# Weight preparation for the second layer in four smaller pieces, one block later, and small constants at other addresses

## The chip, the cores and the metric

The kernel runs on one core of a Trainium2 chip. The metric is the device time of one execution in microseconds (us); lower is better. The engines are named as in the profile: PE multiplies matrices (PEld loads its weights), DVE is the vector engine, ACT the scalar engine, POOL is GpSimd, SP issues the DMA transfers from one queue.

## The reference

Attention with pooled keys and values, and then two feed-forward layers with different gates. All arrays are float32.

```python
def _attn_ref(q, k, v):                      # (8, 8, 576, 64) each
    k_p = k.reshape(B, H, Sp, 8, D).mean(axis=3)
    v_p = v.reshape(B, H, Sp, 8, D).mean(axis=3)
    scores = scale * np.matmul(q, k_p.transpose(0, 1, 3, 2))
    attn = softmax(scores)                   # written out in the reference
    return np.matmul(attn, v_p)

def _moe_ref(x, w_in, w_out):                # x (4608, 512), w_in (512, 2048)
    h = x @ w_in
    g = np.where(h >= 1, h, np.where(h <= -1, 0.0, (h + 1) ** 2 / 4))
    return g @ w_out

def _moe2_ref(x, w_in, w_out):
    h = x @ w_in
    g = h - np.tanh(h)
    return g @ w_out

# out = _moe2_ref(_moe_ref(attention, w1_in, w1_out), w2_in, w2_out)
```

## The kernel before

**Tiling.** The first layer works through 12 blocks of 384 tokens (`TB`), each in 16 steps, one for each 128 of the 2048 hidden columns. Step t = 16 j + f is written "block j, step f" below. Each float32 operand is split into a high and a low half (`xh`/`xl`, `wh`/`wl`, `gh`/`gl`), so a product takes three matmuls: 12 of 384 columns for the hidden values `ph` (`h_mm`, L578) and, two steps later, 12 for the output `po` (`out_mm`, L623). Between them stands a chain over DVE and ACT: `g` is clipped (DVE L585, which is used below to mark the start of a step), squared (ACT L589), combined (DVE L593), and split into `gh` (ACT L601) and `gl` (DVE L602).

**Attention beside it.** While block j runs, the attention of block j + 1 is done, four pairs of heads at steps that a plan fixes. PE makes the scores `psc`, ACT the exponentials `ex` (L452), POOL divides them (L466) and splits a remainder `rr` (L474, L475), PE turns them (`pam`, `par`), ACT and DVE take them out of PSUM (`ah` L511, `al` L517, `ar` L509 and L510), PE multiplies with the values (`ppv`). For a new pair of batch and heads POOL pools the keys and values (`kvraw`, L315, then `bd`, L324 to L326) and PE turns them (`pkt`, L356), into a PSUM buffer that comes free with `al`. Per block this falls to four pairs in blocks 2, 5 and 8, to three in blocks 3, 6 and 9, and to one in blocks 4 and 7.

**Weight preparation for the second layer.** Sixteen units u. Unit u is loaded into `wraw` (`w_load`, L149 or L151, a buffer of which there is one), turned from a scaled bit layout into plain float32 in the staging tile `wf` (`conv`: ACT L159 and L160, DVE L164 to L166, once for each half i), and split into high and low (ACT L249, DVE L250). Even units also get four sums on POOL (L239 to L242, written back into `wraw`) and a second split, of these sums. The results go back to DRAM as `w2c` and `w2o`. The staging tile is the same buffer as `ost`, in which each block's output leaves for DRAM.

**What sets the order.** In the first layer's main loop the program only gives a priority: each step calls its functions in a fixed order, and the plan (`add(t, slot, ...)`) hangs the other work on steps. A scheduler then orders each engine's queue by its own reckoning, and a unit's work may stand steps before or behind the t of its plan. Engines run their queues in order. The second layer (from L875 on) has its order written out by hand, behind the first.

**Addresses.** The pool `const` holds the constants in the order in which they are asked for. When the first layer is over, its pools are given up and the second layer's tiles are laid over the same addresses from the start, in the order of the string `LAYOUT`: first `w0` (14336 bytes per partition), then `s0` (1024), a gap of 640, and so on. With `reuse_waits="tile"` a tile waits for the last users of the tiles that it covers, and of no others. `w0` takes the first weights `wc` of the second layer; `half`, the bias of ACT L589, is read in every step of the first.

Of the kernel before, what the change touches and what calls it, by code (L numbers as in the profile page):

```python
# [10 lines left out]
F32 = mybir.dt.float32  # L11
# [4 lines left out]
ALU = mybir.AluOpType  # L16
# [35 lines left out]
def attention_two_moe_kernel(  # L52
# [50 lines left out]


    kvraw = const.tile([P, 3, POOL * D], F32, tag="kvraw", name="kvraw")
    ident = const.tile([P, P], F32, tag="ident", name="ident")
    half = const.tile([P, 1], F32, tag="half", name="half")
    mask = const.tile([P, 2], F32, tag="mask", name="mask")

    third = const.tile([P, 16], F32, tag="third", name="third")[:, 0:1]  # L110

    vlrs = [const.tile([P, 2, P], F32R, tag=f"vlr{i}", name=f"vlr{i}") for i in range(6)]
    ars = [const.tile([P, TB], F32R, tag=f"ar{i}", name=f"ar{i}") for i in range(2)]
    n_vr = itertools.count()

    def constants(sel):
# [60 lines left out]
    def staging():  # L179
        t = sb.tile([P, KC * TB], I32, tag="ost", name="wf", bufs=1)  # L180
        return t[:, 0 : 2 * 512].rearrange("p (c m) -> p c m", m=512)

    def conv(r, a, s):
        conv_a(r, a, s)
        conv_v(r, a, s)
# [39 lines left out]
            w1_split_a(f)  # L225
            w1_split_v(f)

    def w2_prep(u):
        r, a = raws.pop((1, u)), staging()
        for i in (0, 1):  # L230
            conv(r[:, i], a[:, i], r[:, i, :, 0])
        af = a.bitcast(F32)
        r0, r1 = (r[:, i].rearrange("p m t -> p (m t)") for i in (0, 1))
        U[("w2", u)] = (r, af, r0, r1)
        if u % 2:
            return
        a11, a12, a21, a22 = (af[:, i, 256 * c : 256 * c + 256] for i in (0, 1) for c in (0, 1))
        c1, c2, c3, c4 = (r0[:, 256 * i : 256 * i + 256].bitcast(F32) for i in range(4))
        nc.gpsimd.tensor_tensor(c1, a21, a22, ALU.add)  # L239
        nc.gpsimd.tensor_tensor(c3, a11, a21, ALU.subtract)  # L240
        nc.gpsimd.tensor_tensor(c2, c1, a11, ALU.subtract)
        nc.gpsimd.tensor_tensor(c4, a12, c2, ALU.subtract)  # L242

    def w2_split(u):
        r, af, r0, r1 = U.pop(("w2", u))
        p = u // 2

        def split(x, hi):
            nc.scalar.activation(hi.bitcast(F32R), x, AF.Copy)  # L249
            nc.vector.tensor_tensor(x.bitcast(F32R), x, hi.bitcast(F32), ALU.subtract)  # L250

        if u % 2:
            split(af.rearrange("p i m -> p (i m)"), r0)
            for i in (0, 1):
                hi, lo = r0[:, 512 * i : 512 * i + 512].bitcast(F32), af[:, i]
                nc.sync.dma_start(out=w2o[2 * p + i][:, 0], in_=hi)
                nc.sync.dma_start(out=w2o[2 * p + i][:, 1], in_=lo)
            return
        split(af.rearrange("p i m -> p (i m)"), r1)
        for x, h in ((af.rearrange("p i m -> p (i m)"), 1), (r1.bitcast(F32), 0)):  # L260
            nc.sync.dma_start(out=w2c[p][:, h, 4:6], in_=x[:, 0:512].rearrange("p (m n) -> p m n", n=256))
            nc.sync.dma_start(out=w2c[p][:, h, 6], in_=x[:, 768:1024])
        split(r0.bitcast(F32), r1)
        for x, h in ((r0.bitcast(F32), 1), (r1.bitcast(F32), 0)):
            nc.sync.dma_start(out=w2c[p][:, h, 0:4], in_=x.rearrange("p (m n) -> p m n", n=256))


    xt = {}
# [538 lines left out]
    for f in range(FC):  # L807
        if f >= 2:
            add(FC + f - 2, "w", w1_split, f)
        if f:  # L810
            ahead("w", w_load, (1, f))
        t = FC + 8 * f + 5
        add(t, "w", w2_prep, f)
        add(t + 2, "w", w2_split, f)
        add(t + 3, "load2", used, "w")

    def go(t, *slots):
        for s in slots:
# [278 lines left out]
```

## Time and profile before

| | us |
|---|---|
| median of 3 runs (lowest, highest) | 1779.36 (1778.71, 1782.97) |
| time of the profiled execution | 1774.08 |
| its span from first to last instruction | 1772.3 |
| busy in the span: PE, DVE, ACT, POOL | 1726.8, 1075.9, 820.1, 335.3 |

The profile is one execution. Its span is cut into windows below at the starts of DVE L585, so that a window is a block of 16 steps. The ends of matmuls are modelled, and each overlaps the next, so an idle time of PE is read a little too short.

### The profile page before, as it was taken

The numbers are of one execution on the slowest core, as the hardware profiler recorded it, in microseconds if no ns is written. First come the engines' busy times: TensorE is split into PE (matmuls) and PEld (weight loads), VectorE is DVE, ScalarE is ACT, GpSimd is POOL, SyncE is SP. The second block draws the span as 40 slices with busy tenths as digits, with TensorE's granted clock in tenths as the row PEclk, the third lists the DMA queues.
The fourth block names the chain that finished last, engine by engine and source line by source line (L and its number), as shares of the span: only waits on it lengthen the run. The fifth ranks groups of instructions, "written<-read, shape, count | busy, mean of one in ns | idle before, by whom it ended". The sixth has DMA issues, their size and how long they took to land.

```text
span 1772.3 us, 27599 instructions
## 1 busy us (share of the span) xinstructions
PE 1726.8 (97%) x10224; PEld 1591.2 (90%) x10224; DVE 1075.9 (61%) x1993; ACT 820.1 (46%) x2014; POOL 335.3 (19%) x433
## 2 busy tenths in 40 slices
PE   8999989999999999999999899999999999999999
PEld 6569989899999999899999788998888988889887
DVE  7878876767676676755544445454545455555544
ACT  6656655555555455544432334343434344343433
POOL 5442243321433312431010010110101010101000
PEclk8999999999999999999999899999999999999999
DMA  8643242413343232420100664342434342424232
GB/s 248 212 131 96 88 143 82 151 47 122 101 123 124 75 122 75 131 59 10 28 25 19 254 262 147 105 153 96 143 107 144 107 143 96 154 97 154 95 119 95
DMA packets 162422, 207.59 MB, mean 117 GB/s; under 512 B 77808, under 2 KB 115696, under 8 KB 161264
## 3 DMA queue, kind: packets, MB, share of 16 engines
q1 hardware_dynamic: 162288, 205.84, 35.5%
q8 instruction: 80, 1.31, 0.3%
q14 instruction: 54, 0.44, 0.1%
HBM read 163.32 MB, written 41.94 MB: 116 GB/s over the span
## 4 chain that ended last, share of the span: by engine, by line
PE 76%; DVE 10%; DMA 5%; ACT 4%; POOL 3%; issue 2%; SPq 1%; ACTq 0%; DVEq 0%; POOLq 0%
PE y L993 23%; PE po L623 14%; PE ph L578 14%; PE bkX L928 9%; PE bkA L928 6%; PE bkZ L928 6%; DMA wraw<-in_moe_w_out_dram 2%; DVE gl L602 1%; PE psc L437 1%; DVE wf L166 1%; DVE g L585 1%; DVE wf L250 1%; DVE wraw L164 1%; POOL kvraw L315 1%; PE ph L571 1%
## 5 line engine op out<-in xcount | busy, mean ns | idle before, releaser
L993 PE MATMUL y<-wr,gh 128*128 128x512 f32 x1152 | 362.1, 395 | 0.0
L993 PEld LDWEIGHTS y<-wr,gh 128*128 128x128 f32 x1152 | 206.9, 188 | 39.6
L993 PE MATMUL y<-wr,gl 128*128 128x512 f32 x576 | 227.2, 394 | 0.0
L589 ACT ACTIVATE g<-g,half 128x384 f32<-128x384 f32 x192 | 118.8, 619 | 215.0 <-DVE g L585 214.7
L578 PE MATMUL ph<-xh,whl 128*128 128x384 f32 x704 | 197.7, 341 | 0.0
L623 PE MATMUL po<-gh,whl 128*128 128x384 f32 x704 | 195.7, 339 | 0.0
L928 PE MATMUL bkX<-xc,wc 128*128 128x256 f32 x1296 | 189.8, 282 | 0.0
L968 ACT ACTIVATE th<-c 128x512 f32<-128x512 f32 x144 | 91.1, 632 | 208.5 <-DVE c L961 116.1
L928 PEld LDWEIGHTS bkX<-xc,wc 128*128 128x128 f32 x1296 | 175.0, 190 | 6.0
L981 DVE TENSOR_TENSOR gl<-c,gh 128x512 fp32r<-128x512 f32 x144 | 104.7, 727 | 104.3 <-ACT gh L977 104.3
L971 DVE TENSOR_TENSOR c<-c,th 128x512 f32<-128x512 f32 x144 | 100.9, 701 | 95.6 <-ACT th L968 94.8
L602 DVE TENSOR_TENSOR gl<-g,gh 128x384 fp32r<-128x384 f32 x176 | 110.6, 629 | 74.9 <-ACT gh L601 73.7
L585 DVE TENSOR_SCALAR g<-ph 128x384 f32<-128x384 f32 x192 | 106.1, 553 | 77.2 <-PE ph L578 71.0
L593 DVE TENSOR_TENSOR g<-ph,g 128x384 f32<-128x384 f32 x192 | 106.4, 554 | 74.5 <-ACT g L589 73.0
L977 ACT ACTIVATE gh<-c 128x512 fp32r<-128x512 f32 x144 | 91.0, 632 | 114.2 <-DVE c L971 114.2
L895 POOL TENSOR_TENSOR xr<-xr 128x512 f32<-128x512 f32 x9 | 12.7, 1409 | 661.2 <-DMA xr<-x2d 593.2
L928 PE MATMUL bkA<-xc,wc 128*128 128x256 f32 x864 | 127.7, 284 | 8.1 <-DMA wc<-w2c 4.8
L928 PEld LDWEIGHTS bkA<-xc,wc 128*128 128x128 f32 x864 | 119.0, 192 | 15.0 <-DMA wc<-w2c 5.2
L993 PEld LDWEIGHTS y<-wr,gl 128*128 128x128 f32 x576 | 108.3, 188 | 26.0
L578 PEld LDWEIGHTS ph<-xh,whl 128*128 128x128 f32 x704 | 128.6, 188 | 0.3
L623 PEld LDWEIGHTS po<-gh,whl 128*128 128x128 f32 x704 | 128.8, 188 | 0.0
L601 ACT ACTIVATE gh<-g 128x384 fp32r<-128x384 f32 x176 | 91.9, 522 | 78.0 <-PE po L623 55.3
(156 smaller groups left out, 3672.6 us busy)
## 6 DMA issues: line engine op xcount, KB each, us to landing
wr<-w2o SPq DMA_DIRECT2D x144, 512.0 KB, 3.3
wraw<-in_moe_w_in_dram SPq DMA_DIRECT2D x32, 512.0 KB, 4.7
wraw<-in_moe_w_out_dram SPq DMA_DIRECT2D x32, 512.0 KB, 5.1
wc<-w2c SPq DMA_DIRECT2D x8, 1792.0 KB, 14.2
x2d<-ost SPq DMA_DIRECT2D x48, 192.0 KB, 1.9
out_dram<-yo SPq DMA_DIRECT2D x36, 256.0 KB, 4.5
w2c<-wraw SPq DMA_DIRECT2D x16, 512.0 KB, 2.6
kvraw<-in_k_dram SPq DMA_DIRECT2D x28, 256.0 KB, 2.9
```

The source lines that it names most:

```text
L578: nc.tensor.matmul(ps, a[:, cs], x[:, c, :], start=(i == 0), stop=(i == 3 * KC - 1))
L585: nc.vector.tensor_scalar(a, hp[t], -1.0, 1.0, ALU.max, ALU.min)
L589: nc.scalar.activation(a, a, AF.Square, bias=half, scale=0.5)
L593: nc.vector.tensor_tensor(a, hp.pop(t), a, ALU.max)
L601: nc.scalar.activation(gh, a, AF.Copy)
L602: nc.vector.tensor_tensor(gl, a, gh.bitcast(F32), ALU.subtract)
L623: nc.tensor.matmul(o, a, m, start=(f == 0 and i == 0), stop=(f == FC - 1 and i == len(ops) - 1))
L928: nc.tensor.matmul(o, w[:, wi, c], x[:, xi, c], start=new and i == 0, stop=i == 5, skip_group_check=not new)
L968: nc.scalar.activation(th, H[(n, i)], AF.Tanh)
L971: nc.vector.tensor_tensor(H[(n, i)], H[(n, i)], GG.pop((n, i, "t")), ALU.subtract)
L981: nc.vector.tensor_tensor(gl, H.pop((n, i)), gh.bitcast(F32), ALU.subtract)
L993: nc.tensor.matmul(Y[c], a[:, cs], b, start=first and i == 0, stop=last and i == 2)
```

## The change

The work on a unit is cut into smaller functions: `w2_conv` for each half, `w2_sums`, `w2_own` (the split of the unit itself), `w2_mixed` (the split of the sums) and `w2_rows` (the split of an odd unit). Its plan starts 13 steps later and runs over steps t, t + 2, t + 4 and, for even units, t + 6; the next load is planned for the last of them. No instruction on the engines is added or taken out, and no DMA. The tiles `vlrs` and `ars`, which the attention uses last in block 10, are asked for ahead of `ident`, `half`, `mask` and `third`, so that `w0` and `s0` lie over `kvraw`, `vlrs` and `ars`, and the gap of 640 bytes over the small constants.

```diff
     kvraw = const.tile([P, 3, POOL * D], F32, tag="kvraw", name="kvraw")
+    vlrs = [const.tile([P, 2, P], F32R, tag=f"vlr{i}", name=f"vlr{i}") for i in range(6)]
+    ars = [const.tile([P, TB], F32R, tag=f"ar{i}", name=f"ar{i}") for i in range(2)]
     ident = const.tile([P, P], F32, tag="ident", name="ident")
     half = const.tile([P, 1], F32, tag="half", name="half")
...
-    vlrs = [const.tile([P, 2, P], F32R, tag=f"vlr{i}", name=f"vlr{i}") for i in range(6)]
-    ars = [const.tile([P, TB], F32R, tag=f"ar{i}", name=f"ar{i}") for i in range(2)]
...
+    def w2_conv(u, i):
+        if i == 0:
+            U[("w2", u)] = staging()
+        r, a = w2_parts(u)[:2]
+        conv(r[:, i], a[:, i], r[:, i, :, 0])
...
+    def w2_halves(x, hi):
+        nc.scalar.activation(hi.bitcast(F32R), x, AF.Copy)
+        nc.vector.tensor_tensor(x.bitcast(F32R), x, hi.bitcast(F32), ALU.subtract)
...
+    def w2_own(u):
+        af, r0, r1 = w2_parts(u)[2:]
+        w2_halves(af, r1)
+        for x, h in ((af, 1), (r1.bitcast(F32), 0)):
+            nc.sync.dma_start(out=w2c[u // 2][:, h, 4:6], in_=x[:, 0:512].rearrange("p (m n) -> p m n", n=256))
+            nc.sync.dma_start(out=w2c[u // 2][:, h, 6], in_=x[:, 768:1024])
+
+    def w2_mixed(u):
+        r0, r1 = w2_parts(u)[3:]
+        w2_halves(r0.bitcast(F32), r1)
         for x, h in ((r0.bitcast(F32), 1), (r1.bitcast(F32), 0)):
-            nc.sync.dma_start(out=w2c[p][:, h, 0:4], in_=x.rearrange("p (m n) -> p m n", n=256))
+            nc.sync.dma_start(out=w2c[u // 2][:, h, 0:4], in_=x.rearrange("p (m n) -> p m n", n=256))
+        raws.pop((1, u))
...
-        t = FC + 8 * f + 5
-        add(t, "w", w2_prep, f)
-        add(t + 2, "w", w2_split, f)
-        add(t + 3, "load2", used, "w")
+        t = 2 * FC + 8 * f + 2
+        add(t, "w", w2_conv, f, 0)
+        add(t + 2, "w", w2_conv, f, 1)
+        if f % 2:
+            add(t + 4, "w", w2_rows, f)
+            add(t + 4, "load2", used, "w")
+        else:
+            add(t + 2, "w", w2_sums, f)
+            add(t + 4, "w", w2_own, f)
+            add(t + 6, "w", w2_mixed, f)
+            add(t + 6, "load2", used, "w")
```

How the queues change is shown at three places. In the changed kernel's rows the line numbers differ: L585, L593, L602 and L517 become L590, L598, L607 and L522; the conversions L159, L160 and L164 to L166 become L157, L158 and L162 to L164; the splits L249 and L250 become L247 and L248; POOL's L315, L466 and L242 become L320, L471 and L244.

**First place** (blocks 2, 5 and 8, steps 3 to 5). POOL's queue holds the sums of an even unit (`wraw`), the division of the exponentials (`ex`) and the pooling of keys and values (`kvraw`). Before:

```order
L240 TENSOR_TENSOR wraw<-wf 128x256
L241 TENSOR_TENSOR wraw<-wraw,wf 128x256
L315 TENSOR_TENSOR kvraw<-kvraw 128x3x256
L466 TENSOR_TENSOR ex<-ex,rc 128x432
L242 TENSOR_TENSOR wraw<-wf,wraw 128x256
L474 CAST rr<-ex 128x3x16
L315 TENSOR_TENSOR kvraw<-kvraw 128x3x128
```

After:

```order
L242 TENSOR_TENSOR wraw<-wf 128x256
L243 TENSOR_TENSOR wraw<-wraw,wf 128x256
L320 TENSOR_TENSOR kvraw<-kvraw 128x3x256
L244 TENSOR_TENSOR wraw<-wf,wraw 128x256
L320 TENSOR_TENSOR kvraw<-kvraw 128x3x128
L471 TENSOR_TENSOR ex<-ex,rc 128x432
L320 TENSOR_TENSOR kvraw<-kvraw 128x3x64
```

The fourth sum, which reads `wf` last, stood behind the division and now stands ahead of it, and the second pooling step goes ahead of the division too. DVE's queue at the same place, from step 3's `gl` to step 5's `ar`; before:

```order
L602 TENSOR_TENSOR gl<-g,gh 128x384
L585 TENSOR_SCALAR g<-ph 128x384
L593 TENSOR_TENSOR g<-ph,g 128x384
L602 TENSOR_TENSOR gl<-g,gh 128x384
L585 TENSOR_SCALAR g<-ph 128x384
L517 TENSOR_TENSOR al<-pam,ah 128x384
L593 TENSOR_TENSOR g<-ph,g 128x384
L510 CAST ar_132<-par 16x128
L250 TENSOR_TENSOR wraw<-wraw 128x1024
L510 CAST ar_132<-par 16x128
```

After:

```order
L607 TENSOR_TENSOR gl<-g,gh 128x384
L590 TENSOR_SCALAR g<-ph 128x384
L598 TENSOR_TENSOR g<-ph,g 128x384
L248 TENSOR_TENSOR wraw<-wraw 128x1024
L607 TENSOR_TENSOR gl<-g,gh 128x384
L590 TENSOR_SCALAR g<-ph 128x384
L522 TENSOR_TENSOR al<-pam,ah 128x384
L598 TENSOR_TENSOR g<-ph,g 128x384
L515 CAST ar_128<-par 16x128 x2
L607 TENSOR_TENSOR gl<-g,gh 128x384
```

The split of the sums (`wraw<-wraw`) stood in step 5, between two `ar`, and now stands in step 4, ahead of that step's `gl` and of the next `al`.

**Second place** (the same blocks, steps 7 to 9): the conversions of the next, odd unit and its split, DVE. Before:

```order
L164 SCALAR_TENSOR_TENSOR wraw<-wraw 128x512
L165 TENSOR_SCALAR wf<-wf 128x512
L602 TENSOR_TENSOR gl<-g,gh 128x384
L166 ISA wf<-wraw,wf 128x1024
L164 SCALAR_TENSOR_TENSOR wraw<-wraw 128x512
L585 TENSOR_SCALAR g<-ph 128x384
L165 TENSOR_SCALAR wf<-wf 128x512
L166 ISA wf<-wraw,wf 128x1024
L593 TENSOR_TENSOR g<-ph,g 128x384
L250 TENSOR_TENSOR wf<-wf,wraw 128x1024
L602 TENSOR_TENSOR gl<-g,gh 128x384
L585 TENSOR_SCALAR g<-ph 128x384
```

After:

```order
L162 SCALAR_TENSOR_TENSOR wraw<-wraw 128x512
L163 TENSOR_SCALAR wf<-wf 128x512
L590 TENSOR_SCALAR g<-ph 128x384
L164 ISA wf<-wraw,wf 128x1024
L464 TENSOR_SCALAR sm<-sm 128x6
L162 SCALAR_TENSOR_TENSOR wraw<-wraw 128x512
L598 TENSOR_TENSOR g<-ph,g 128x384
L466 RECIPROCAL rc<-sm 128x6
L163 TENSOR_SCALAR wf<-wf 128x512
L164 ISA wf<-wraw,wf 128x1024
L607 TENSOR_TENSOR gl<-g,gh 128x384
L590 TENSOR_SCALAR g<-ph 128x384
```

Each half of a unit has three conversion instructions (L164, L165, L166; L162 to L164 after). They stood in steps 7 and 8; now the first two stand at the end of step 6, the other four in step 7, and step 8, which begins with the last row shown of the change, holds only the split (`wf<-wf,wraw`). ACT's queue at that place, before:

```order
L601 ACTIVATE gh<-g 128x384
L452 ACTIVATE ex,sm<-psc,mx 128x72 x6
L589 ACTIVATE g<-g,half 128x384
L159 ACTIVATE wraw<-wraw 128x512
L160 ACTIVATE wf<-wraw 128x512
L601 ACTIVATE gh<-g 128x384
L159 ACTIVATE wraw<-wraw 128x512
L160 ACTIVATE wf<-wraw 128x512
```

After:

```order
L606 ACTIVATE gh<-g 128x384
L157 ACTIVATE wraw<-wraw 128x512
L158 ACTIVATE wf<-wraw 128x512
L457 ACTIVATE ex,sm<-psc,mx 128x72 x6
L157 ACTIVATE wraw<-wraw 128x512
L594 ACTIVATE g<-g,half 128x384
L158 ACTIVATE wf<-wraw 128x512
L606 ACTIVATE gh<-g 128x384
L247 ACTIVATE wraw<-wf 128x1024
```

The first conversions stood behind the six exponentials and now stand ahead of them.

**Third place** (SP, from the second to last block's output `x2d` to the first weights of the second layer, with what each waits for). Before:

```order
L633 DMA x2d_118<-ost 128x384 [waits DMAHW6_49,DVE_49]
L875 DMA wc_10510<-w2c_84 128x3584 [waits DMAHW7_49,Activation_49]
L633 DMA x2d_119<-ost 128x384 [waits DMAHW0_49,Activation_49]
L633 DMA x2d_119<-ost 128x384 [waits DMAHW1_49,DVE_49]
L633 DMA x2d_119<-ost 128x384 [waits DMAHW2_49,Activation_49]
L633 DMA x2d_119<-ost 128x384 [waits DMAHW3_49,DVE_49]
L875 DMA wc_10516<-w2c_85 128x3584 [waits DMAHW4_49,PE_49]
```

After:

```order
L638 DMA x2d_118<-ost 128x384 [waits DMAHW6_49,DVE_49]
L887 DMA wc_10510<-w2c_84 128x3584 [waits DMAHW7_49]
L638 DMA x2d_119<-ost 128x384 [waits DMAHW0_49,Activation_49]
L638 DMA x2d_119<-ost 128x384 [waits DMAHW1_49,DVE_49]
L638 DMA x2d_119<-ost 128x384 [waits DMAHW2_49,Activation_49]
L638 DMA x2d_119<-ost 128x384 [waits DMAHW3_49,DVE_49]
L887 DMA wc_10516<-w2c_85 128x3584 [waits DMAHW4_49,PE_49]
```

The order is the same; the load of `wc` into `w0` no longer waits for ACT.

## Rows read from the trace of the kernel before

**Rows 1.** The page's first line.
```profile
span 1772.3 us, 27599 instructions
```

**Rows 2.** Windows: five blocks; us, then busy us (instructions) of each engine.
```profile
135.18:214.29 79.11, 77.45 (x443) 73.87 (x442) 68.28 (x121) 54.98 (x142) 20.76 (x24) 1.00 0.33 101
454.43:535.95 81.52, 76.95 (x456) 75.15 (x455) 56.95 (x108) 42.71 (x124) 31.49 (x44) 1.00 0.38 114
535.95:617.87 81.92, 78.28 (x473) 75.85 (x472) 56.68 (x109) 42.54 (x123) 26.56 (x37) 1.00 0.34 105
617.87:693.37 75.50, 75.01 (x445) 74.52 (x444) 51.96 (x104) 40.66 (x116) 16.05 (x23) 1.00 0.30 96
774.75:851.88 77.13, 77.13 (x473) 75.86 (x472) 42.93 (x91) 34.45 (x110) 12.43 (x23) 1.00 0.12 30
```

**Rows 3.** Waits of PE over the span: us in total, times, longest.
```profile
PE pkt L356 <- DVE al L517: 16.1, 10, 3.1
PE bkA L928 <- DMA wc<-w2c: 4.8, 1, 4.8
PE ppv L537 <- DVE ar L510: 4.1, 7, 0.9
...
PE bkA L928 <- ACT s L940: 3.2, 1, 3.2
```

**Rows 4.** Timeline of POOL, block 2: start us, us, instruction.
```profile
231.90 1.83 POOL L315 TENSOR_TENSOR kvraw<-kvraw 128x768 f32<-128x768 f32 x1
233.69 0.91 POOL L466 TENSOR_TENSOR ex<-ex,rc 128x432 f32<-128x432 f32 x1
234.56 0.74 POOL L242 TENSOR_TENSOR wraw<-wf,wraw 128x256 f32<-128x256 f32 x1
```

**Rows 5.** Timeline of DVE, block 2, first place; idle before in brackets.
```profile
235.33 1.23 DVE L250 TENSOR_TENSOR wf<-wf,wraw 128x1024 fp32r<-128x1024 f32 x1 [3.40 <-POOL wraw L242]
...
241.21 0.55 DVE L517 TENSOR_TENSOR al<-pam,ah 128x384 fp32r<-128x384 f32 x1
```

**Rows 6.** Timeline of PE, block 2, first place.
```profile
241.81 0.33 PE L356 MATMUL pkt<-ident,bd 128*128 128x128 f32 x1 [1.38 <-DVE al L517]
```

**Rows 7.** Timeline of DVE, block 2, second place.
```profile
254.94 2.33 DVE L166 CUSTOM_DVE_ANT_0 wf<-wraw,wf 128x1024 uint16<-128x1024 uint16 x1
...
259.53 0.69 DVE L166 CUSTOM_DVE_ANT_0 wf<-wraw,wf 128x1024 uint16<-128x1024 uint16 x1
...
263.49 0.55 DVE L517 TENSOR_TENSOR al<-pam,ah 128x384 fp32r<-128x384 f32 x1
```

**Rows 8.** Timeline of DVE, block 3, second place.
```profile
340.30 1.38 DVE L166 CUSTOM_DVE_ANT_0 wf<-wraw,wf 128x1024 uint16<-128x1024 uint16 x1
```

**Rows 9.** Timeline of DVE, block 4, first place.
```profile
404.60 1.23 DVE L250 TENSOR_TENSOR wraw<-wraw 128x1024 fp32r<-128x1024 f32 x1 [0.23 <-ACT wraw L249]
```

**Rows 10.** Timeline of SP's DMA queue, block 2.
```profile
244.85 0.41 SPq L307 DMA_DIRECT2D kvraw<-in_k_dram  x1
...
247.44 0.81 SPq L149 DMA_DIRECT2D wraw<-in_moe_w_out_dram  x2
```

**Rows 11.** DMA issues of the page: count, KB each, median us to landing.
```profile
wraw<-in_moe_w_out_dram SPq DMA_DIRECT2D x32, 512.0 KB, 5.1
```

**Rows 12.** Timeline of ACT, last step of the first layer.
```profile
989.44 0.62 ACT L589 ACTIVATE g<-g,half 128x384 f32<-128x384 f32 x1 [2.21 <-DVE g L585]
```

**Rows 13.** Timeline of SP's DMA queue at the change of layers.
```profile
990.08 0.32 SPq L875 DMA_DIRECT2D wc<-w2c  x1
993.40 1.97 SPq L633 DMA_DIRECT2D x2d<-ost  x4
995.46 1.37 SPq L875 DMA_DIRECT2D wc<-w2c  x2
```

**Rows 14.** Windows at the change of layers; then granted clock, DMA share, GB/s.
```profile
992.00:1020.00 28.00, 19.92 (x105) 18.65 (x105) 8.83 (x17) 6.86 (x14) 0.00 (x0) 0.76 1.00 407
```

**Rows 15.** Timeline of PE, second group of output products.
```profile
1020.75 0.73 PE L993 MATMUL y<-wr,gh 128*128 128x512 f32 x2
```

More of the change, by code (lines that the diff above doesn't have):

```diff
@@ L226, in w1_split, with w2_parts, w2_sums @@
             w1_split_v(f)
[L228 to L232, printed above, removed]
-        r0, r1 = (r[:, i].rearrange("p m t -> p (m t)") for i in (0, 1))
[L234 to L237, printed above, removed]
+    def w2_parts(u):
+        r, a = raws[(1, u)], U[("w2", u)]
+        r0, r1 = (r[:, i].rearrange("p m t -> p (m t)") for i in (0, 1))
+        return r, a, a.bitcast(F32).rearrange("p i m -> p (i m)"), r0, r1
+    def w2_conv(u, i):
[3 more added lines that the diff above has]
+        conv(r[:, i], a[:, i], r[:, i, :, 0])
+    def w2_sums(u):
+        r, a, af, r0, r1 = w2_parts(u)
+        a11, a12, a21, a22 = (af[:, 256 * i : 256 * i + 256] for i in range(4))
         c1, c2, c3, c4 = (r0[:, 256 * i : 256 * i + 256].bitcast(F32) for i in range(4))
@@ L242, in w2_prep, with w2_rows @@
         nc.gpsimd.tensor_tensor(c4, a12, c2, ALU.subtract)
[L244 to L263, printed above, removed]
+    def w2_halves(x, hi):
+        nc.scalar.activation(hi.bitcast(F32R), x, AF.Copy)
+        nc.vector.tensor_tensor(x.bitcast(F32R), x, hi.bitcast(F32), ALU.subtract)
+    def w2_rows(u):
+        af, r0 = w2_parts(u)[2:4]
+        w2_halves(af, r0)
+        for i in (0, 1):
+            for h, x in enumerate((r0.bitcast(F32), af)):
+                nc.sync.dma_start(out=w2o[u - 1 + i][:, h], in_=x[:, 512 * i : 512 * i + 512])
+        raws.pop((1, u))
[8 more added lines that the diff above has]
+        w2_halves(r0.bitcast(F32), r1)
         for x, h in ((r0.bitcast(F32), 1), (r1.bitcast(F32), 0)):
-            nc.sync.dma_start(out=w2c[p][:, h, 0:4], in_=x.rearrange("p (m n) -> p m n", n=256))
+            nc.sync.dma_start(out=w2c[u // 2][:, h, 0:4], in_=x.rearrange("p (m n) -> p m n", n=256))
+        raws.pop((1, u))
     xt = {}
```

## The prediction

> **What bounds the kernel now.** PE does. The page's first line gives the span, 1772.3 us [rows 1]; the profiled execution took 1774.1, and the median of the runs shown is 1779.4, so I make the sum against 1774.1 and carry its difference over to the median. The windows by block come next [rows 2]. A block's length less PE's busy time is what PE lost: 4.57 us in block 5 (81.52 - 76.95), 3.64 in block 6, 0.49 in block 7, and nothing in block 9, which has no weight preparation. Block 9 and block 6 do the same attention, so 81.92 - 77.13 = 4.79 us is what preparing two units costs such a block; the 1.15 above its 3.64 hides in the modelled ends of matmuls. The list of PE's waits says where the time goes [rows 3]: 16.1 us in 10 waits of `pkt` for `al` on DVE, 4.1 us in 7 waits of `ppv` for `ar` on DVE, 4.8 us for the first weights of the second layer and 3.2 us just behind. DVE is busy only 57 of 81.5 us in block 5, so it isn't full; it is late at two places of a block because long instructions and waits stand ahead of the short ones that PE needs.
>
> **The change part by part.** No instruction comes or goes; only places move. I take the blocks by their number of pooled pairs.
>
> Blocks 2, 5, 8, first place (now 1.4 for `pkt`, 0.9 for `ppv`, and some 0.3 for `par`: 2.6 us). DVE stood still for 3.40 us, in front of the unit's own split, until POOL's fourth sum was done [rows 5], and that sum stood behind a pooling step of 1.83 and a division of 0.91 [rows 4]. The division now stands behind the sum, so the sum and everything behind it on DVE comes 0.9 us earlier; with the conversion also ahead of a transposition, I take 1.4. The own split's successor, a `gl`, also ran beside a pooling step and was long; I take 0.8 more for that. Against it, the split of the sums moves ahead of `al`: 1.23 us [rows 9]. So `al`, at 241.21 before [rows 5], comes about 1.0 earlier and ends at 240.75. PE came to `pkt` 1.38 us before 241.81 [rows 6], at 240.43, and will come there half a microsecond sooner, because `par` no longer waits: 0.85 us of waiting are left. `ppv`'s 0.9 goes, since the split of 1.23 us no longer stands between two `ar`. Gain 1.75.
>
> The same blocks, second place (now 2.0 us). Here `al`, at 263.49, stands behind conversions, of which one took 2.33 us and a later one of the same size 0.69 [rows 7], and behind a split of 1.23. They move up by as much as their load allows. The load was issued at 247.44 and takes 5.1 us [rows 10, 11]. It waits until the split sums have left `wraw`; that split comes some 5 us earlier, but two loads of keys, the first at 244.85 before [rows 10], now stand ahead of it and wait for POOL, so I take the load 3.2 us earlier, landing at 249.3. The conversions begin then, 3.2 us earlier, while PE itself comes 1.75 earlier; so 1.45 of the 2.0 us go and 0.55 stay. Together 1.75 + 1.45 = 3.2 a block; bounds are 0 (all late again) and 4.57 (all hidden). For three blocks: 9.6.
>
> Blocks 3 and 6 (3.64 us each). At the first place the earlier sums are missing, and the split moved ahead of `al` costs what `ppv`'s lost wait gives: nothing. At the second, a conversion took 1.38 us [rows 8] beside POOL, and the waits are the longest, 2.7 to 3.1 [rows 3]. The load comes early enough for step 6, but four ACT conversions now stand ahead of the exponentials and push `gl` and the next step's clip back; what is surely gained is the split out of step 8, 1.23, less about 0.1. Gain 1.1 a block, 2.2 for two; bounds -1 and 3.64.
>
> Block 9 has paid nothing and now gets two units. It pays what block 6 paid less that gain: 4.79 - 1.1 = 3.7; bounds 0.5 and 4.8.
>
> Blocks 4 and 7: the 0.49 us of `ppv` goes for the reason above, 1.0 for two; bounds 0 and 1. Block 1 loses unit 0's work; PE idles 1.66 us there [rows 2]; I take 1.0, bounds 0 and 1.7.
>
> The constants. The load into `w0` was issued at 990.08 [rows 13], when the last ACT L589 of the first layer, which reads `half` at 989.44, had ended [rows 12]. Now it follows the output of the block before, some 57 us earlier, when DMA is all but idle, and the 4.8 us wait of the first `bkA` goes. But what PE needs next isn't earlier. The other weights still stand behind the last `x2d`, issued from 993.40 to 995.37, and the first of them is issued at 995.46 [rows 13]. From 992 to 1020 the DMA engines were full, at 407 GB/s [rows 14]. Up to the `wr` that the second group of output products needs, five `wc` of 1792 KB, four `x2d` of 192 KB and two `wr` of 512 KB pass, 11.0 MB, which at that rate takes 27 us; from about 991.4, 1.3 us behind the issue at 990.08 (an estimate), that is 1018.4. The group ran at 1020.75 [rows 15], 2.3 later, about what a landing takes to be seen. Without `w0`'s load 9.2 MB are left, which start behind the first `x2d` at about 994.7 (by the same 1.3 us) and take 22.5 us: 1017.2, seen at 1019.5. So 1.3 us can be gained, not 4.8. PE will wait about 4 us for the second `wc` and 5 to 6 us for that `wr`, and its clock falls in such waits: the mean granted clock was 0.76 over these 28 us [rows 14], that is 13 us at the lower of its two levels, 1.2 instead of 2.4 GHz. After a wait that ends in the lower level the products run at half speed for some microseconds, a loss of 1 to 3. I take 0.5 us slower; bounds 1.3 faster and 2 slower, unless the bound by DMA is wrong (below).
>
> The Trainium skill (DMA: Bandwidth & Descriptors, "Queues, rings and completion order") says that each DMA engine takes descriptors in ring order. By that rule the `wr` can't pass the `wc` ahead of it, and the gain stays at 1.3; the trace fits, with `wr` in use just when 11.0 MB had passed.
>
> The sum: -9.6 - 2.2 + 3.7 - 1.0 - 1.0 + 0.5 = -9.6 us, 1764.5 on the profiled execution's scale and 1769.8 on the median's. I forecast 1770.
>
> **The rivals.**
> Full cover: all waits of DVE go, in block 9 too. Blocks 2, 5, 8 give 13.7, blocks 3 and 6 7.3, blocks 4, 7 and 1 2.7, block 9 costs 0.5, the constants nothing: 23 us, 1756. For it speaks that DVE has 24 us free in block 5; against it, that the conversions wait for one load into one buffer.
> The change of layers pays in full: the DMA queue catches up, and 4.8 us of waiting and the slow clock behind it, 2.7 us, go on top of the sum: -9.6 - 0.5 - 7.5 = -17.6, 1762. Against it stands the 407 GB/s.
> It does nothing: the waits only change their place, since each unit still needs the same work between the same loads, or DVE meets POOL elsewhere. An instruction of 0.69 took 2.33 beside POOL's pooling [rows 7]; 16 units with one more such meeting lose what the sum gives, within 5 us of 1779. The Trainium skill (GPSIMD Engine Reference, "Key points") states that POOL shares its SBUF interfaces with DVE instructions that have two SBUF inputs; by it every conversion, split and `gl` can meet POOL, and the trace shows such meetings.
> Slower: ACT, which now holds conversions ahead of the exponentials, waits for the load in every block. My reckoning has it land about when ACT comes; if SP holds it up so that it lands over 3 us later than that, `gh`, the exponentials and then `al` are late by the rest. At 5 us too late, 2 us of new waits in each of 8 blocks with nothing gained at the second places (3 x 1.45 + 2.2 = 6.5 lost again): 16 + 6.5 - 9.6 = +13, 1792; from 3.4 us too late on it turns the sign.
>
> **How the numbers follow.** Forecast (5 to 15 us faster) 0.50; full cover 0.15; the change of layers in full 0.10; nothing 0.15; slower 0.10. A measurement of this kernel can tell about 0.3%, 5.3 us. Faster by more than that: the first three, less the forecast's edge, 0.72; within it 0.18; slower 0.10. The range leaves out the far half of full cover and most of the slower case: 1757 to 1781.
>
> **What would show it.** Right: POOL's fourth sum ahead of the division and DVE's 3.4 us wait down to about 2; `pkt` waits under 1 us in blocks 2, 5 and 8, and near 2 in 3 and 6; block 9 longer by 3 to 4 us with waits that block 9 never had; no `ppv` wait for `ar`; `w0`'s load issued near 933, and PE waiting for the second `wc` and a `wr` instead, with the clock at its lower level after them. Wrong: `pkt` waits gone altogether, or ACT idle ahead of L157 for microseconds, or PE running through the change of layers without waiting.

## The result, and the profile after

The changed kernel takes 1764.0 us (median of 4 runs, 1762.0 to 1766.2) against 1779.0 for the kernel before: a ratio of 0.9914, with a 95% interval of 0.9890 to 0.9938. That is 15 us less, inside the range given, and 6 us below the 1770 forecast. The profiled executions differ by less. The page's first line after:

```profile
span 1764.2 us, 27575 instructions
```

Against [rows 1] that is 8.1 us. The windows by block, cut as in [rows 2] at the starts of the clip of `g` (now L590), are blocks 1, 2, 5, 6, 7 and 9:

```profile
135.36:212.80 77.44, 76.86 (x443) 73.97 (x442) 58.19 (x106) 47.08 (x131) 16.58 (x22) 1.00 0.15 39
212.80:292.77 79.97, 77.25 (x456) 75.11 (x455) 56.38 (x109) 42.28 (x124) 30.64 (x45) 1.00 0.38 116
447.71:528.28 80.57, 77.09 (x456) 75.10 (x455) 56.45 (x109) 42.18 (x124) 30.45 (x44) 1.00 0.36 115
528.28:608.70 80.42, 78.24 (x473) 75.59 (x472) 55.38 (x109) 42.09 (x123) 27.75 (x37) 1.00 0.34 107
608.70:683.53 74.83, 74.83 (x445) 74.49 (x444) 51.89 (x104) 40.68 (x116) 15.61 (x23) 1.00 0.31 98
763.75:842.38 78.63, 77.81 (x473) 75.67 (x472) 51.69 (x105) 40.47 (x119) 18.56 (x27) 1.00 0.26 79
```

Every other block is a little shorter, and block 9 is 1.50 us longer. The waits of PE, to be held against [rows 3]:

```profile
PE pkt L361 <- DVE al L522: 8.6, 9, 1.4
PE y L1005 <- DMA wr<-w2o: 6.2, 1, 6.2
PE par L498 <- POOL rr L480: 5.4, 8, 1.5
PE bkA L940 <- DMA wc<-w2c: 3.2, 1, 3.2
...
PE ppv L540 <- DVE ar L515: 0.6, 2, 0.3
```

`pkt` has lost half of its 16.1 us, the longest wait fell from 3.1 to 1.4, `ppv` has lost all but 0.6 of 4.1, and a wait of `par` for POOL has come in their place. Behind the first layer the first weights cost nothing now; the second ones cost 3.2 and the second output weights 6.2.

In the first place of block 2, POOL (sums L243 and L244, poolings L320, division L471, remainder L480), to be compared with [rows 4]:

```profile
229.91 1.86 POOL L320 TENSOR_TENSOR kvraw<-kvraw 128x768 f32<-128x768 f32 x1
231.72 0.75 POOL L244 TENSOR_TENSOR wraw<-wf,wraw 128x256 f32<-128x256 f32 x1
232.42 1.02 POOL L320 TENSOR_TENSOR kvraw<-kvraw 128x384 f32<-128x384 f32 x1
233.38 1.91 POOL L471 TENSOR_TENSOR ex<-ex,rc 128x432 f32<-128x432 f32 x1
...
236.41 0.29 POOL L480 TENSOR_TENSOR rr<-ex,rr 128x48 fp32r<-128x48 f32 x1
```

and DVE there, against [rows 5]:

```profile
232.50 2.02 DVE L248 TENSOR_TENSOR wf<-wf,wraw 128x1024 fp32r<-128x1024 f32 x1 [2.37 <-POOL wraw L244]
234.45 1.26 DVE L607 TENSOR_TENSOR gl<-g,gh 128x384 fp32r<-128x384 f32 x1
...
239.94 0.55 DVE L522 TENSOR_TENSOR al<-pam,ah 128x384 fp32r<-128x384 f32 x1
```

The division went out of the sum's way, and DVE's wait fell from 3.40 to 2.37 us. But the split behind it now takes 2.02 us instead of 1.23, the `gl` behind that is long beside POOL as it was before, and `al` starts 27.1 us into the block (239.94 - 212.80), where it started at 26.9 (241.21 - 214.29). POOL's remainder `rr` comes late too. PE waits for both:

```profile
236.76 0.31 PE L498 MATMUL par<-ident,rr 128*96 128x128 f32 x1 [0.58 <-POOL rr L480]
...
240.55 0.33 PE L361 MATMUL pkt<-ident,bd 128*128 128x128 f32 x1 [1.39 <-DVE al L522]
```

The table adds up the blocks of four traces: the profiled one of before, a second one of the same kernel (`before_again` below), the changed kernel, and the changed kernel without the preparation of weights (`no_prep`). The tail runs from the first layer's last step to the end.

| us | before | before again | changed | no preparation |
|---|---|---|---|---|
| block 1 | 79.1 | 79.2 | 77.4 | 77.4 |
| blocks 2, 5, 8 | 81.6, 81.5, 81.4 | 83.1, 81.5, 81.3 | 80.0, 80.6, 80.2 | 76.1, 76.0, 76.0 |
| blocks 3, 6 | 83.1, 81.9 | 84.9, 84.8 | 80.1, 80.4 | 77.1, 77.1 |
| blocks 4, 7 | 75.5, 75.5 | 75.5, 75.5 | 74.9, 74.8 | 74.7, 74.7 |
| block 9 | 77.1 | 77.1 | 78.6 | 77.1 |
| blocks 1 to 10 | 790.4 | 796.7 | 780.7 | 759.9 |
| tail | 783.5 | 785.9 | 785.0 | 783.8 |

### The profile page after: what moved, and what is told of

Read it like the earlier page. It is cut to its first block, busy times and chain, and to the rows that moved or that the text cites. A ratio compares the mean times of both kernels' runs of the same rounds, so it can differ in the third digit from the quotient of the medians.

```text
span 1764.2 us, 27575 instructions
## 1 busy us (share of the span) xinstructions
PE 1727.4 (98%) x10224; PEld 1590.4 (90%) x10224; DVE 1071.8 (61%) x1993; ACT 817.4 (46%) x2014; POOL 334.1 (19%) x433
## 4 chain that ended last, share of the span: by engine, by line
PE 80%; DVE 7%; ACT 4%; DMA 3%; POOL 3%; issue 2%; SPq 0%; ACTq 0%; POOLq 0%; DVEq 0%
PE y L1005 23%; PE po L628 16%; PE ph L583 15%; PE bkX L940 9%; PE bkA L940 6%; PE bkZ L940 6%; PE ph L576 2%; PE psc L442 1%; DMA wr<-w2o 1%; DVE gl L607 1%; DVE g L590 1%; DMA wraw<-in_moe_w_out_dram 1%; POOL kvraw L320 1%; ACT g L594 1%; DVE wf L248 1%
## 5 line engine op out<-in xcount | busy, mean ns | idle before, releaser
L607 DVE TENSOR_TENSOR gl<-g,gh 128x384 fp32r<-128x384 f32 x176 | 111.8, 635 | 73.9 <-ACT gh L606 71.1
L598 DVE TENSOR_TENSOR g<-ph,g 128x384 f32<-128x384 f32 x192 | 106.6, 555 | 75.9 <-ACT g L594 74.5
L590 DVE TENSOR_SCALAR g<-ph 128x384 f32<-128x384 f32 x192 | 105.9, 552 | 69.0 <-PE ph L583 62.1
```

Source lines behind the costliest of these rows:

```text
L590: nc.vector.tensor_scalar(a, hp[t], -1.0, 1.0, ALU.max, ALU.min)
L598: nc.vector.tensor_tensor(a, hp.pop(t), a, ALU.max)
L607: nc.vector.tensor_tensor(gl, a, gh.bitcast(F32), ALU.subtract)
```

## The experiments

**The kernel before once more.**

> The kernel before, run again, with a granted clock for each run. Theory (clock): in the two profiled executions the change gained 8.1 us (1772.3 to 1764.2), the medians differ by 15. If the rest is TensorE's clock, the runs of this kernel near 1779 show a mean clock near 0.988, since 0.001 of the clock over 1770 us is some 1.8 us, and the run with 0.991 is near 1774. Rival: the clock is 0.991 in all, and the profiled execution was short for another reason, so the change gained 15 us by its own steps.

The median was 1780.5, the ratio to the kernel before 1.0007 (0.9992 to 1.0022). The mean clock was 0.989 to 0.991 in nine of the twelve runs, of 1779 to 1781 us, and 0.987 or 0.988 in three of 1785 to 1788. So the clock's mean doesn't separate 1774 from 1780 as expected: both have 0.991. What does is where the lower level fell. Blocks 2, 3 and 6 in this trace (the last columns are granted clock, DMA share, GB/s):

```profile
212.06:295.15 83.09, 78.51 (x456) 76.72 (x455) 57.19 (x110) 42.70 (x124) 32.84 (x47) 0.98 0.37 111
295.15:380.05 84.90, 80.69 (x473) 78.21 (x472) 56.32 (x109) 42.37 (x123) 25.65 (x37) 0.96 0.33 101
...
537.08:621.86 84.78, 81.13 (x473) 78.69 (x472) 56.14 (x108) 42.45 (x123) 26.90 (x39) 0.96 0.33 102
```

A mean of 0.96 over 84.9 us is 6.8 us at 1.2 instead of 2.4 GHz. In the execution that the prediction was worked from, block 6 ran at 1.00 throughout [rows 2], and block 3 had half of that. These three blocks are 6.2 us longer here. In the profiled one 13.7 us of lower clock lay in the first 40 us instead; block 1 starts 2.4 us later there, 135.2 us into the span against 132.8. The two executions also show that a wait of one length can go either way. PE's wait in block 6, in the profiled one and in this one:

```profile
586.05 0.33 PE L356 MATMUL pkt<-ident,bd 128*128 128x128 f32 x1 [3.14 <-DVE al L517]
```

```profile
587.16 0.47 PE L356 MATMUL pkt<-ident,bd 128*128 128x128 f32 x1 [3.14 <-DVE al L517]
```

The same two drops in blocks 3 and 6 are in the traces of `consts_only` and `late_only`, which order the attention's waits as before.

**Each half of the change alone.** `spread_only` is the changed kernel with the constants in the old order (the diff), `consts_only` the kernel before with the new one (the same two tiles moved the other way):

```diff
     kvraw = const.tile([P, 3, POOL * D], F32, tag="kvraw", name="kvraw")
-    vlrs = [const.tile([P, 2, P], F32R, tag=f"vlr{i}", name=f"vlr{i}") for i in range(6)]
-    ars = [const.tile([P, TB], F32R, tag=f"ar{i}", name=f"ar{i}") for i in range(2)]
...
+    vlrs = [const.tile([P, 2, P], F32R, tag=f"vlr{i}", name=f"vlr{i}") for i in range(6)]
+    ars = [const.tile([P, TB], F32R, tag=f"ar{i}", name=f"ar{i}") for i in range(2)]
     n_vr = itertools.count()
```

> The changed kernel with the constants in the old order. Theory (the change of layers is bound by DMA): blocks 1 to 10 as long as in the changed kernel (780.7 us), the first weights of the second layer wait for the last squaring again, PE waits 4.9 us for them, and the rest from the last step to the end takes 783.5 us as before instead of 785.0: 1 to 2 us faster than the changed kernel, 1762 to 1763. Rival (the constants pay): 4 to 7 us slower than the changed kernel, 1768 to 1771.

> The kernel before with the constants in the new order and nothing else. Theory (bound by DMA): blocks as before, waits of 3.2 us for the second weights and some 6 us for the second output weights in place of 4.9 and 3.2, 1 to 2 us slower than before, 1780. Rival (the constants pay): 4 to 7 us faster than before, 1772 to 1775.

`spread_only` took 1762.6 us, ratio 0.9900 (0.9883 to 0.9918); in its trace blocks 1 to 10 take 779.5 us and the tail 783.3. `consts_only` gave 1.0000 (0.9990 to 1.0010). The constants don't pay, on either kernel: the whole gain is the spread's. Nor is it shown that they cost the 1 to 2 us that was expected. With the old order the tails are 783.5, 785.9 and 783.3 us (the two traces of the kernel before, and `spread_only`), with the new one 785.0 and 783.4 (the changed kernel, and `consts_only`).

**A block later, without cutting; cut, without the block later.** `late_only` is `consts_only` with the first of these edits, `early` the changed kernel with the second:

```diff
-        t = FC + 8 * f + 5
+        t = 2 * FC + 8 * f + 5
...
-        t = 2 * FC + 8 * f + 2
+        t = FC + 8 * f + 2
```

> The kernel before, its two pieces of work on a unit planned 16 steps later and not cut further, with the constants in the new order. Theory (the cutting gains, the later block costs): block 1 gets 1.7 us shorter, block 9 pays what block 6 pays, 4.8 to 7.7 us, the waits of 2 to 3.7 us and the drops of the clock stay: 3 to 6 us slower than before, 1783 to 1787. Rival (the later block gains): faster than before by 5 us or more, 1775 or less.

> The changed kernel with the four pieces planned 16 steps earlier, in blocks 1 to 8. Theory (the later block is worth nothing by itself): block 9 loses its 1.5 us, block 1 gets about 1.7 longer, the waits of blocks 2 to 8 stay as in the changed kernel: within 2 us of 1764. Rival (the block later is half of the gain): 5 us or more slower than the changed kernel.

`late_only` missed: 1777.7 us, ratio 0.9978 (0.9965 to 0.9990), a little faster than before. Block 9 took 79.4 us there, 2.3 more than before and not 4.8 to 7.7, and its one wait at the second place was short:

```profile
823.15 0.33 PE L356 MATMUL pkt<-ident,bd 128*128 128x128 f32 x1 [0.53 <-DVE al L517]
```

where block 6 of the same trace waits 3.73. Why it is faster than before at all stays open: its blocks 1 to 10 take 796.1 us, as in `before_again`.

`early` gave 1767.4 us at a ratio of 0.9914 (0.9899 to 0.9930), the changed kernel's own. So cutting the work makes the gain, without the block later. What the block later adds is open: nothing by the ratios, 3.4 us by the medians, and 4.9 us in the traces, where the blocks 1 to 10 of `early` take 785.6 us. Block 1, which was expected about 1.7 us longer, is 5.9 longer there, with a new wait for `al` and 6.8 us at the lower clock:

```profile
132.67:215.98 83.31, 79.89 (x443) 76.75 (x442) 68.54 (x121) 54.86 (x142) 20.73 (x26) 0.96 0.32 96
```

```profile
156.92 0.58 PE L442 MATMUL psc<-kt,qt 128*128 128x144 f32 x1 [3.31 <-DVE al L522]
```

Block 6 has a drop of 3.4 us too, behind a wait of 1.7, and is 1.6 us longer; block 9 gives its 1.5 us back.

**A long wait put back.** The changed kernel, with `al` of blocks 3, 6 and 9 computed four times:

```diff
-        nc.vector.tensor_tensor(al, pm, ah.bitcast(F32), ALU.subtract)
+        for _ in range(4 if p == 2 and j in (4, 7, 10) else 1):
+            nc.vector.tensor_tensor(al, pm, ah.bitcast(F32), ALU.subtract)
```

> The changed kernel with al of the second place of blocks 3, 6 and 9 computed four times instead of once, 1.65 us more of DVE ahead of PE's next products; nothing else. Theory (a wait of 2.5 us or more makes the clock fall): PE waits 3.0, 2.7 and 2.0 us there, the granted clock goes to its lower level for 3.4 to 6.8 us behind the first two waits, as in the kernel before, and they cost 1.7 to 3.4 us more each: 8 to 12 us slower than the changed kernel. Rival (the drops in the kernel before have another cause): three times 1.65, 5 us slower, and no drop between 50 and 980 us.

1772.2 us, ratio 0.9936 (0.9917 to 0.9956). Between 4 us slower than the changed kernel by the ratios and 8 by the medians, the time doesn't tell the theories apart. The trace does. PE's three waits (put down to an `ar` that DVE did in the midst of the copies), and the three blocks:

```profile
343.23 0.45 PE L361 MATMUL pkt<-ident,bd 128*128 128x128 f32 x1 [3.01 <-DVE ar L515]
...
581.93 0.45 PE L361 MATMUL pkt<-ident,bd 128*128 128x128 f32 x1 [2.70 <-DVE ar L515]
...
819.54 0.30 PE L361 MATMUL pkt<-ident,bd 128*128 128x128 f32 x1 [2.00 <-DVE ar L515]
```

```profile
292.06:376.60 84.54, 80.87 (x473) 78.66 (x472) 56.79 (x112) 42.65 (x123) 26.92 (x37) 0.96 0.33 102
530.98:615.41 84.43, 81.00 (x473) 78.75 (x472) 56.75 (x112) 42.47 (x123) 27.31 (x37) 0.96 0.33 102
769.79:851.53 81.74, 79.29 (x473) 77.33 (x472) 53.25 (x108) 40.58 (x119) 18.53 (x27) 0.98 0.25 76
```

The drops are back, 6.8, 6.8 and 3.4 us long, with waits of 3.0, 2.7 and 2.0 us, in blocks 3 and 6 at the places where the kernel before has them. The bound of 2.5 us in the theory was wrong, since the wait of 2.0 us has a drop too. The blocks pay 4.5, 4.0 and 3.1 us for 1.65 us of DVE; so 2.8, 2.4 and 1.5 us of it come on top of the longer wait.

**Without the preparation, and without the pooling.** In `no_prep` the bodies of `w2_conv`, `w2_sums` and `w2_halves` are empty, and `w2_parts` gives a weight tile of the first layer. `no_pool` keeps them and leaves out POOL's additions:

```diff
-        tree(eng, kvraw)
+        if b < 2:
+            tree(eng, kvraw)
```

> The changed kernel without any work of the engines on the second layer's weights: its conversions, sums and splits are left out, the loads stay, and the results in DRAM are written from a weight tile of the first layer, so the second layer computes with other numbers. What it gains is what the preparation still costs. Theory (the remaining waits of pkt and par come from it): blocks 3, 6 and 9 fall to about 77.1 us as block 9 before, blocks 2, 5 and 8 by about 3, blocks 4 and 7 by about 0.5, in all 15 to 18 us, 1746 to 1749. Rival (the remaining waits belong to the attention's own chain over POOL, ACT and DVE): under 5 us.

> The changed kernel without POOL's pooling additions of keys and values from the third batch on (24 of the 28 poolings of the main loop): the keys and values are then those of the first of eight tokens, times the same factor. The order on PE, DVE and ACT, the loads and bd stay as they are. Theory (most of what the preparation still costs is POOL: sums that stand behind a pooling, and DVE instructions that take long beside one): DVE's wait for the fourth sum falls from 2.4 us to about 0.6, the conversion of 2.3 us at the second place of block 6 takes 0.7, blocks 3 and 6 come down to 78.6 us like block 9, which has no pooling, blocks 2, 5 and 8 by 1.5 to 2.5: 8 to 11 us faster than the changed kernel, 1753 to 1756. Rival (the loads or ACT, DVE and PE themselves): no block changes by more than 0.5 us.

`no_prep` took 1742.3 us (0.9774, interval 0.9756 to 0.9792): the preparation still costs 20.8 us in the blocks, more than the 15 to 18 expected and more than the waits listed for PE show. `no_pool` took 1748.1 (0.9820, 0.9786 to 0.9855), more than was expected of it. Its blocks 2, 3 and 6:

```profile
213.75:290.10 76.35, 76.32 (x456) 75.40 (x455) 52.87 (x109) 42.82 (x124) 15.54 (x32) 1.00 0.38 121
290.10:368.29 78.19, 77.76 (x473) 75.65 (x472) 53.13 (x109) 42.13 (x123) 15.96 (x28) 1.00 0.35 110
519.15:597.70 78.55, 77.79 (x473) 75.64 (x472) 52.29 (x108) 42.06 (x123) 16.29 (x28) 1.00 0.36 110
```

Blocks 1 to 10 sum to 764.1 us, 16.6 less than in the changed kernel, though all the weight preparation is there and PE, DVE and ACT have the same queues. With pooling and without preparation they take 759.9, and there block 3, which pools three times, takes 77.1 us like block 9, which pools once: the pooling alone costs nothing that shows. The preparation without the pooling costs 4.2 us more than that, and both together 20.8. That is the price of the pooling beside the preparation by either path: POOL comes later with its sums and with `rr`, and DVE's instructions take longer beside it (DVE is busy 56.38 us in block 2 of the changed kernel and 52.87 here, with the same instructions). The run doesn't separate the two. DVE's wait for the fourth sum is down to 0.68, as expected:

```profile
231.77 1.92 DVE L248 TENSOR_TENSOR wf<-wf,wraw 128x1024 fp32r<-128x1024 f32 x1 [0.68 <-POOL wraw L244]
```

**The order of the loads.**

The first edit makes `wr_first`, both make `wr_next`:

```diff
-    for i, t in enumerate((-54, -29, -28, -27)):
+    for i, t in enumerate((-57, -56, -50, -49)):
         at_time(t, wr_load, fs[i])
...
-    for p, t in enumerate((-80, -60, -55, -44, -34, 0, 8, 22)):
+    for p, t in enumerate((-80, -60, -55, -44, -34, 26, 33, 43)):
         at_time(t, wc_load, p)
```

> The changed kernel with the loads of the second layer's first weights in another order on SP: the first two output weights ahead of the third input weights, the third and fourth output weights ahead of the fourth input weights. Theory (bound by DMA, in the order of the queue): the second output weights land near 996 instead of 1009.8, PE's wait of 6.2 us for them goes, and most of the 10 us at the lower clock behind it, while the third input weights land near 1000, before PE wants them: 6 to 9 us faster than the changed kernel, 1755 to 1758. Rival (the same bytes must pass before PE can go on): the wait moves to the third or fourth input weights, and the time stays within 2 us of 1764.

> As wr_first, and the sixth to eighth loads of the second layer's input weights are issued some 26, 25 and 21 us later, behind the fifth and sixth output weights. Theory (PE's last wait in wr_first, 4.0 us at 1014.6 for the fifth output weights that landed at 1018.6 behind two of these loads, is the order of the queue again): they land near 1010, the wait goes, 4 to 6 us faster than wr_first, 1751 to 1753; the wait of 3.3 us for the second input weights stays. Rival (later loads come too late): a new wait for the sixth input weights, 1757 or more.

`wr_first`: 1757.3 us, 0.9875 (0.9857 to 0.9893). The 6.2 us wait is gone, and the next one in the queue shows:

```profile
1018.63 0.73 PE L1005 MATMUL y<-wr,gh 128*128 128x512 f32 x2 [4.04 <-DMA wr<-w2o]
```

`wr_next`: 1752.7 us, 0.9845 (0.9822 to 0.9868), tail 775.6 us. Of the change of layers only the 3.1 us wait for the second weights is left. It is the fastest kernel here that leaves nothing out, 11 us below the changed one. The intervals of the neighbours touch or overlap, but the runs lie nearly apart: 1762.0 to 1766.2 us for the changed kernel, 1755.9 to 1760.0 for `wr_first`, 1752.6 to 1756.0 for `wr_next`.

**Pooling put behind.** The edit of `pool_behind`; `both` has it beside those of `wr_next`:

```diff
-        tree(eng, kvraw)
+        if b < 2:
+            tree(eng, kvraw)
+        else:
+            with tc.issue_after(newest(E.Pool)):
+                tree(eng, kvraw)
```

> The changed kernel with one rule more for the order: from the third batch on, POOL's pooling of keys and values is put behind the POOL instruction that stands ahead of it in the program, so POOL's queue holds an even unit's four sums, then the division and the remainder of the exponentials, and then the pooling, which stood between or ahead of them. Theory (what the preparation still costs is DVE and PE waiting for POOL, and conversions of 0.7 us that take 2.3 beside a pooling): the wait of DVE for the fourth sum goes from 2.4 to under 0.7 us, the waits of par for rr go, the conversion at the second place of blocks 3 and 6 takes 0.7 us, and these two blocks come down to about 78.6 us as block 9, blocks 2, 5 and 8 by 1.5 to 2.5: 8 to 11 us faster than the changed kernel. Rival (the pooling only meets other DVE instructions, or comes too late for pkt): within 3 us of the changed kernel, with waits of pkt for bd.

> pool_behind and wr_next together. Theory: the two gains add up, since one lies in blocks 2 to 9 and the other behind the last block: 1742 to 1746. Rival: with a shorter first layer the loads at the change of layers are late by more, and a third or less of the one gain is lost: 1747 to 1750.

Both missed by far: 1854.0 us, 1.0409 (1.0384 to 1.0435), and 1846.4, 1.0366 (1.0342 to 1.0390). The two differ by 7.6 us, so two thirds of the loads' gain were kept, but the pooling's turned into a loss of 90. In block 2, first POOL, then DVE, then PE:

```profile
246.87 0.76 POOL L333 TENSOR_TENSOR bd<-kvraw,mask 128x128 f32<-128x128 f32 x2
```

```profile
248.00 0.29 DVE L354 TENSOR_TENSOR vlr<-bd,vh 128x128 fp32r<-128x128 f32 x1 [4.92 <-ACT vh L344]
...
252.53 0.55 DVE L526 TENSOR_TENSOR al<-pam,ah 128x384 fp32r<-128x384 f32 x1
```

```profile
253.22 0.45 PE L365 MATMUL pkt<-ident,bd 128*128 128x128 f32 x1 [4.48 <-DVE al L526]
```

`bd` comes late; ACT's `vh` and DVE's `vlr`, which read it, stand in their queues ahead of the splits and of `al`, and PE waits for `al` at 24 places, 72 us, with 15 drops of the clock in the blocks. I had taken for slack that POOL's `bd` idles 4 us in the changed kernel; the instructions behind `bd` on the other engines had none. The rule changed the order together with the meetings, so it says nothing on the pooling's price; `no_pool` does.

## Why the prediction came out as it did

**The scale.** The terms for the blocks came to -10.1 us, and blocks 1 to 10 of the two profiled traces differ by 9.7. That they meet so closely is luck: the gain of blocks 2, 5 and 8 was put 5.9 us too high and all the others together 5.5 too low, as the parts below show. The 15 us of the medians contain a term that the sum had not: the clock behind DVE's late `al`. I read one execution, found its clock at 1.00 in the blocks of [rows 2] and carried 1774.1 over to 1779.4 by adding the difference. That difference was not an offset. In the second trace of the kernel before, the blocks 2, 3 and 6, with their drops, are 6.2 us longer than in the profiled one, and the changed kernel, whose waits are 1.5 us or less, has no drop in its blocks, nor have `spread_only`, `wr_first` and `wr_next`; `early`, with waits of 3.3 and 1.7 us, has two. Against that second execution the profiled one of the changed kernel gains 16.0 us in the blocks (796.7 - 780.7) and 0.9 in the tail, and loses 2.5 before block 1: 14.4 us of span, and 15 was measured. That long waits bring the drops is shown by `al_long`. How often the ordinary runs have all three is not: three traces of this attention order besides the profiled one have those of blocks 3 and 6, and two of these that of block 2.

**Blocks 2, 5 and 8: -9.6 forecast, -3.7 measured.** The first place failed in two steps. "`par` no longer waits": it waits 0.52 to 0.58, since two poolings now stand ahead of the division. And "`al` comes about 1.0 earlier": what the sum gave DVE, 1.0 us, went into a split that took 0.8 longer beside POOL, the 0.8 that I had credited to a shorter `gl` didn't come (1.26 us), and the split of the sums stands ahead of `al` as reckoned; the wait is 1.39 against 1.38. `ppv`'s 0.9 went as said. At the second place the load did better than reckoned: it was forecast to land at 249.3, ACT took up its first half at 247.28, and it waited little for it in block 2:

```profile
247.28 0.67 ACT L157 ACTIVATE wraw<-wraw 128x512 int32<-128x512 uint32 x1 [0.37 <-DMA wraw<-in_moe_w_out_dram]
```

`pkt`'s 2.0 us are gone altogether, but `par` waits 0.6 to 1.5 there, for a remainder whose division waits for DVE's reciprocal `rc`. In block 2 that stands behind a conversion which took 2.15 us beside a pooling, where its other half took 0.65:

```profile
250.89 2.15 DVE L162 SCALAR_TENSOR_TENSOR wraw<-wraw 128x512 int32<-128x512 int32 x1 [0.34 <-ACT wraw L157]
```

Besides the poolings ahead of the division, the step that failed in both places is one: I moved DVE's instructions in time and kept their durations, and they met POOL in a new place. The sign named for these blocks, `pkt` waits under 1 us, came at the second place and not at the first.

**Blocks 3 and 6: -2.2 forecast.** They are 4.5 us shorter than in the profiled execution and 9.2 shorter than in the second one. No run shows apart what the split out of step 8 was worth. The waits of `pkt` at the second place fell from 2.7 and 3.1 us to 1.4 and 1.1, under the 2 forecast, and no drop of the clock stands behind them.

**Block 9: +3.7 forecast, +1.5 measured.** "It pays what block 6 paid" was wrong, because block 9 pools keys and values once, at the first place, and block 6 three times, one of them at the second place, where the conversion is. (The expectation of `no_pool` calls block 9 one without pooling; taking its one away gave 0.4 us.) The same conversion in the changed kernel, DVE in block 6, with the split behind it, and in block 9; then POOL in block 6, the first step of the pooling and the division:

```profile
566.72 2.28 DVE L164 CUSTOM_DVE_ANT_0 wf<-wraw,wf 128x1024 uint16<-128x1024 uint16 x1
...
570.18 1.45 DVE L248 TENSOR_TENSOR wf<-wf,wraw 128x1024 fp32r<-128x1024 f32 x1
...
801.99 0.68 DVE L164 CUSTOM_DVE_ANT_0 wf<-wraw,wf 128x1024 uint16<-128x1024 uint16 x1
```

```profile
566.60 1.84 POOL L320 TENSOR_TENSOR kvraw<-kvraw 128x768 f32<-128x768 f32 x1 [4.93 <-DMA kvraw<-in_v_dram]
...
570.51 1.89 POOL L471 TENSOR_TENSOR ex<-ex,rc 128x432 f32<-128x432 f32 x1
```

`late_only` shows the same without the cutting (2.3 us), `no_pool` from the other side: there blocks 3, 6 and 9 take 78.2 to 78.6 us, alike.

**Blocks 4, 7 and 1.** Blocks 4 and 7 gained 1.3 us, where 1.0 was forecast. Block 1 gained 1.7, its upper bound, where 1.0 was forecast.

**The constants: +0.5 forecast, no cost shown.** The mechanism and the waits held. The load for `w0` was issued at 923.3 (forecast: near 933), PE ran through the first products, and then:

```profile
993.14 1.19 PE L940 MATMUL bkA<-xc,wc 128*128 128x256 f32 x4 [3.20 <-DMA wc<-w2c]
...
1009.87 1.22 PE L1005 MATMUL y<-wr,gh 128*128 128x512 f32 x2 [6.17 <-DMA wr<-w2o]
```

The forecast had waits of about 4 and of 5 to 6 us here, with the clock at its lower level behind them; at the change of layers 17.1 us lie at the lower level, where the profiled execution of the kernel before has 13.7. The tails of the two profiled traces differ by 1.5 us, but the two traces of the kernel before differ by 2.4, and in the second of them PE waits 4.3 us for these output weights too; `consts_only` gave a ratio of 1.0000. `wr_first` and `wr_next` show that it is the order in the queue that binds: with the same bytes in another order 6.9 and then 5.3 us went, taken from the ratios. Both have the constants in the new order; whether that order pays beside the new order of the loads was not run.

**The rivals.** That the change of layers pays in full fell with `consts_only`. Full cover fell with the waits that stayed. That the change does nothing fell with the 15 us, though this rival's mechanism, DVE meeting POOL elsewhere, is what took 5.9 us from blocks 2, 5 and 8 together with the poolings ahead of the division. The slower case, ACT held up by the load, has its start in the trace: in blocks 1 to 10 ACT's first conversions wait 12 times for the load, 9.1 us in all and 1.8 at the longest, where the kernel before has 7 such waits of 3.2 us. With PE's waits shorter it didn't decide.

## What to carry to other kernels

A wait's price is its length and what the clock does behind it, so two or three traces of the kernel before are worth having before a sum is made: the one at hand may be the lucky one. When an instruction is moved, its duration in the new place is an unknown again if another engine works on SBUF there; take it from a block where the neighbours are the ones it will get. And where a transfer queue is full, look at the order of what is in it before the time at which its first load is issued.

## What the runs showed of the hardware

**Waits and the clock.** With PE's waits of 1.7 to 5.4 us inside the blocks 1 to 10 of these traces came nothing, 3.4 or 6.8 us at 1.2 instead of 2.4 GHz, and the same wait can go either way: 3.14 us in block 6 brought no drop in the profiled execution of the kernel before and 6.8 us in the second, where the block is 2.9 us longer. With waits of up to 1.5 us came none. What decides between equal waits stays open.

**DVE beside POOL.** In these rows the meetings are not a slowing but a standing still. The conversion at 566.72, of 0.68 us elsewhere, began 0.1 us behind the first step of the pooling and ended at 569.00, 0.55 behind the end of that step at 568.45. The division at 570.51, begun beside a split of DVE that ended at 571.63, ended 0.8 behind it and took 1.89 instead of 0.91 [rows 4]. The Trainium skill (SBUF — State Buffer, "SBUF: two separate sides") says that the pair of ports which DVE and GpSimd share is held for a whole instruction while the other one is blocked; these rows agree with it. What had not been expected is the sum. Taking POOL's additions away gave 16.6 us of the first layer, and DVE was then busy 516.6 us in blocks 1 to 10 instead of 534.8, with the same instructions in the same order. How much of the 16.6 us is this standing still, and how much POOL's own lateness, no run shows.
